# Splitting every whole-array product and transpose into two column halves

## The chip, the cores and the metric

One core of one Trainium2 chip runs the whole kernel in one launch. The metric is the device time of an execution in microseconds. Times of the kernel before are the median of three runs; the profile is of one further execution.

## What is computed

Retention-like attention (scores weighted by a power of a constant of each head, no softmax) over 8 batches, 8 heads, 576 positions and 64 numbers a head, and on its output a feed-forward layer with a SoLU activation and a normalisation over 1024 hidden columns:

```python
scores = scale * np.matmul(q, k.transpose(0, 1, 3, 2))
gamma = 1.0 - 2.0 ** (-5.0 - np.arange(H))
Dmat = np.where(rel >= 0, gamma[:, None, None] ** rel, 0.0)
attn = np.matmul(scores * Dmat, v)            # -> x: 4608 tokens x 512

h = x @ w_in                                   # 512 -> 1024
e = np.exp(h - h.max(-1, keepdims=True))
solu = h * e / (e.sum(-1, keepdims=True) + 1e-9)
ln = (solu - mu) / np.sqrt(var + 1e-6) * g_ln
out = ln @ w_out                               # 1024 -> 512
```

## The kernel before

**Tiles.** The 4608 tokens are 36 chunks of 128. A batch is four chunks and half of a fifth; the fifth of two batches share one chunk, so every ninth chunk is such a shared one. The decay is split into a factor of the row and one of the column, which are multiplied into q and v, and a chunk's past comes from a running state of 64 x 64 numbers a head, so that a chunk needs its own scores and one product with the state.

**Steps.** Each chunk n passes through small functions with names of two letters. Those of TensorE are:

- `tq`, `tr` (L232, L256): transposes of q, and of k in early chunks, 128 x 128 each, into PSUM (`tp`, `tr`); later chunks have k transposed by a DMA (`kd`, L241)
- `sc` (L290): scores, two heads at a time, each in one half of the array's rows (operands of 64 partitions)
- `kv` (L314) and `av` (L365): the state's new part `kp`, and scores times v, `x`; two heads at a time, each in one half of the array's columns (outputs of 64 partitions). These two already have the form that the change gives to others
- `fs` (L380): adds the product of q with the state to `x`
- `m1`, `mr` (L412, L400): `h`, 8 matmuls of 512 columns in two accumulations of four
- `tu` (L495): 8 transposes of the activated `u` into `lp`
- `m2` (L515): `o`, 8 matmuls of 512 columns in one accumulation
- `hm`, `ht`, `h2` (L538, L588, L619): the last chunk's `h`, transposes and `o`, in two parts each; `mm` (L721) a mean over w_out, `wu` (L645) four matmuls ahead of use

The others: POOL scales and converts q, v and k (L210, L199, L171) and makes the state in two forms (`dk` L341, `d3` L353), and computes the normalisation's factor `rs` (L477 to L487). VectorE adds to the state (`ad`, `t`, L327 and L329), masks the scores (`ret`, L303), takes the maximum (`nm`, L422) and forms `u` (L437). ScalarE copies out of PSUM (L171), takes the exponential (`e`, L428), squares (`sq`, L465) and scales the output (`o_sb`, L523).

**Order.** Nothing is scheduled by a planner: three strings of tokens (START, LOOP, END) name the steps in program order, and each engine takes its own in that order. LOOP stands for one step of a software pipeline over the chunks; on TensorE it runs `tr` (chunk + 2), `tu` (- 2), `m1`, `kv` (+ 1), `av` (+ 1), `sc` (+ 2), `fs` (+ 1), `m2` (- 2). A fourth string, BANKS, says which of four PSUM banks each product takes; `h` has two buffers of its own. SP's queue issues the loads some six chunks ahead, the stores, and the DMA transposes.

Of the kernel before, what the change touches and what calls it, by code (L numbers as in the profile page):

```python
# [13 lines left out]
P = 128  # L14
# [79 lines left out]
def kernel(  # L94
# [10 lines left out]
    nc = tc.nc  # L105
# [3 lines left out]
    NF = DFF // P  # L109
# [35 lines left out]
    ident = const.tile([P, P], F16, name="ident")  # L145
    mhalf = const.tile([P, 1], FP, name="mhalf")
    warm = const.tile([P, 512], F16, name="warm")
    ones = const.tile([P, P], F16, name="ones")
# [5 lines left out]
    w_in16 = const.tile([P, 4, DFF], F16, name="w_in16")  # L154
    w_out16 = const.tile([P, NF, DM], F16, name="w_out16")
# [8 lines left out]
    def bank(shape, dtype, name):  # L164
        return ps.tile(shape, dtype, tag="b" + next(banks), name=name)

    ENG = {"a": nc.scalar, "v": nc.vector, "g": nc.gpsimd}
    T = {}
# [2 lines left out]
        (engine.copy if engine is nc.scalar else engine.tensor_copy)(out=out, in_=in_)  # L171


    def quads(n):

        return n != NCH - 2

    def ld(n):

        for key, src in (("qf", q), ("kf", k), ("vf", v)):  # L180
            dst = load.tile([P, H, D], FP, name=key, bufs=6 if key == "kf" else 7)
            for pp, b, s0 in rows(n):
                m = pp.stop - pp.start
                if key == "qf" and quads(n):
                    nc.sync.dma_start(
                        out=dst[pp].rearrange("p (h a) d -> p h (a d)", h=2),
                        in_=src[b, :, s0 : s0 + m, :].rearrange(
                            "(g h) (t a) d -> t g h (a d)", h=2, a=4
                        ),
                    )  # L190
                    continue
                nc.sync.dma_start(
                    out=dst[pp], in_=src[b, :, s0 : s0 + m, :].rearrange("h p d -> p h d")
                )
            T[key, n] = dst
# [9 lines left out]
    def cq(n, e="g"):  # L205
        if not quads(n):
            return scaled(n, "qf", "q16", gq, ENG[e])
        table = gqm if chunks[n][1] == 4 else gqt
        dst = half.tile([P, H, D], F16, name="q16", bufs=5)
        ENG[e].tensor_tensor(  # L210
            out=dst.rearrange("p (a h) d -> p h a d", h=2),
            in0=T.pop(("qf", n)).rearrange("p (h a) d -> p h a d", h=2),
            in1=table.rearrange("p (h a) -> p h a", h=2).unsqueeze(3).to_broadcast([P, 2, 4, D]),
            op=ALU.mult,
        )
        T["q16", n] = dst
# [9 lines left out]
    def tq(n):  # L226

        tp = bank([P, 2, 4, P], F16, "tp")
        for i, src in enumerate((T.pop(("q16", n)), T["k16", n])):
            s2 = src.rearrange("p h d -> p (h d)")  # L230
            for hp in range(4):
                nc.tensor.transpose(  # L232
                    out=tp[:, i, hp], in_=s2[:, hp * P : (hp + 1) * P], identity=ident
                )
        T["tp", n] = tp

    def kd(n):
# [12 lines left out]
    def tr(n):  # L250
        if chunks[n][1] == 4 or n < BY_DMA:
            return tq(n)
        tp = bank([P, 4, P], F16, "tr")
        s2 = T.pop(("q16", n)).rearrange("p h d -> p (h d)")
        for hp in range(4):
            nc.tensor.transpose(  # L256
                out=tp[:, hp], in_=s2[:, hp * P : (hp + 1) * P], identity=ident
            )
        T["tp", n] = tp

    def er(n, e="a"):
# [4 lines left out]
    def turned(engine, n, out, tp):  # L266

        if not quads(n):
            return copy(engine, out, tp)
        copy(  # L270
            engine, out.rearrange("p g (t a) -> p g t a", a=4),
            tp.rearrange("p a (t g) -> p g t a", g=4),
        )
# [98 lines left out]
    def fs(n):  # L372

        bs, c = chunks[n]
        qkT = T.pop(("qkT", n))
        s16 = [T.pop(("s16", b, c)) for b in bs] if c > 0 else []
        w = P // len(bs)
        for hp in range(4):
            for i, s in enumerate(s16):
                nc.tensor.matmul(  # L380
                    out=T["x", n][:, hp, i * w : (i + 1) * w],
                    lhsT=s[:, hp].rearrange("p e d -> p (e d)"),
                    rhs=qkT[:, 0, hp, i * w : (i + 1) * w],
                    start=False, stop=i == len(s16) - 1, skip_group_check=True,
                )
        T["xs", n] = T.pop(("x", n))

# [5 lines left out]
    def mr(n, d):  # L393

        d = int(d)
        done = T.get(("rows", n), 0)
        if done == 0:
            T["h", n] = ps_h.tile([P, DFF], FP, tag="h", name="h")
        for i in range(2):
            nc.tensor.matmul(  # L400
                out=T["h", n][:, i * 512 : (i + 1) * 512], lhsT=T["xT", n][:, d],
                rhs=w_in16[:, d, i * 512 : (i + 1) * 512], start=done == 0, stop=done == 3,
            )
        T["rows", n] = done + 1

    def m1(n):

        xT = T.pop(("xT", n))
        h = ps_h.tile([P, DFF], FP, tag="h", name="h")
        for i in range(2):  # L410
            for d in range(4):
                nc.tensor.matmul(  # L412
                    out=h[:, i * 512 : (i + 1) * 512], lhsT=xT[:, d],
                    rhs=w_in16[:, d, i * 512 : (i + 1) * 512], start=d == 0, stop=d == 3,
                )
        T["h", n] = h

    def mx(n):
# [71 lines left out]
    def tu(n):  # L490

        u = T.pop(("u", n))
        lp = bank([P, NF, P], F16, "lp")
        for c in range(NF):
            nc.tensor.transpose(out=lp[:, c], in_=u[:, c * P : (c + 1) * P], identity=ident)  # L495
        T["lp", n] = lp

    def du(n):
# [9 lines left out]
    def m2(n):  # L508

        uT = T.pop(("uT", n))  # L510
        o = bank([P, DM], FP, "o")
        assert T["w_out"] == NF and (n < PLAIN or T["w_cen"] == NF)
        w = w_out16 if n < PLAIN else T["w_c"]
        for c in range(NF):
            nc.tensor.matmul(  # L515
                out=o, lhsT=uT[:, c], rhs=w[:, c], start=c == 0, stop=c == NF - 1
            )
        T["o", n] = o

    def st(n):  # L520
# [10 lines left out]
    def hm(n, i):  # L531

        if i == "0":
            T["hx", n] = T.pop(("xT", n))
        i = int(i)
        h = bank([P, 512], FP, "hh")
        for d in range(4):
            nc.tensor.matmul(  # L538
                out=h, lhsT=T["hx", n][:, d], rhs=w_in16[:, d, i * 512 : (i + 1) * 512],
                start=d == 0, stop=d == 3,  # L540
            )
        T["hh", n, i] = h

    def hx(n, i):
# [38 lines left out]
    def ht(n, i):  # L583
        i = int(i)
        lp = bank([P, 4, P], F16, "lph")
        u = T.pop(("hu", n, i))
        for c in range(4):
            nc.tensor.transpose(out=lp[:, c], in_=u[:, c * P : (c + 1) * P], identity=ident)  # L588
        T["hlp", n, i] = lp

    def he(n, i, e="v"):
# [22 lines left out]
    def h2(n, i):  # L614

        w = slice(256 * int(i), 256 * int(i) + 256)
        o = bank([P, 256], FP, "oh")
        for c in range(NF):
            nc.tensor.matmul(  # L619
                out=o, lhsT=T["huT", n, c // 4][:, c % 4], rhs=T["w_c"][:, c, w], start=c == 0,  # L620
                stop=c == NF - 1,
            )
        T["ho", n, i] = o

    def hw(n, i, e):
# [15 lines left out]
    def wu(_, count):  # L641

        w = bank([P, 512], FP, "w")
        for _ in range(int(count)):
            nc.tensor.matmul(  # L645
                out=w, lhsT=warm[:, 0:P], rhs=warm, start=True, stop=True, skip_group_check=True
            )

    def c1(_):
        nc.scalar.dma_start(out=small, in_=nc.inline_tensor(small_np, name="small_c").ap())  # L650
# [65 lines left out]
    def mm(_):  # L716

        assert T["w_out"] == NF
        T["mean"] = bank([P, DM], FP, "mean")
        for c in range(NF):  # L720
            nc.tensor.matmul(  # L721
                out=T["mean"], lhsT=ones, rhs=w_out16[:, c], start=c == 0, stop=c == NF - 1
            )

    def mc(_, e):
        copy(ENG[e], warm, T.pop("mean"))
# [51 lines left out]
```

## Time and profile before

| | us |
|---|---|
| median of three runs (lowest, highest) | 217.87 (217.39, 219.24) |
| the profiled execution | 218.18 |
| its span in the profile | 216.5 |
| busy: PE, PE weight loads | 197.4, 110.8 |
| busy: DVE, ACT, POOL | 180.8, 167.1, 173.6 |

The profiled execution is 1.7 us longer than its span; that lies around the profiled part. PE is TensorE's matmuls, PEld its weight loads, which overlap the matmuls; DVE is VectorE, ACT ScalarE, POOL GpSimd, SP SyncE. A matmul's duration runs to the end of its drain, so matmuls of one group overlap in the rows: 128*128 with 512 columns lasts 379 ns, while the next one starts 216 ns after it. A shape such as 128*64 128x512 says that 128 rows and 64 columns of the array are used and that 512 columns are streamed.

### The profile page before, as it was taken

Reading aid. Unit: us, or ns where it says so; the run is one execution under the profiler, and the core shown is the slowest. Engines: PE = TensorE matmul, PEld = TensorE weight load, DVE = VectorE, ACT = ScalarE, POOL = GpSimd, SP = SyncE. Lnnn points to the kernel's source line nnn. Section 1 sums busy time; section 2 is a strip of 40 time slices with the busy share of each in tenths; the row PEclk is TensorE's granted clock in tenths of the full one; section 3 lists DMA queues with packets and bytes.
Section 4 is the critical chain, followed back from the end, with each engine's and each line's share of the span. In section 5 each row is a group of like instructions: output and inputs, shape, how many; then the busy total and the mean of one; then the engine's idle time right before and its main releaser. Section 6 shows DMA issues by size and latency. Waiting matters only on the chain.

```text
span 216.5 us, 5376 instructions
## 1 busy us (share of the span) xinstructions
PE 197.4 (91%) x1989; PEld 110.8 (51%) x1989; DVE 180.8 (84%) x289; ACT 167.1 (77%) x279; POOL 173.6 (80%) x275
## 2 busy tenths in 40 slices
PE   0379889896999999999999999999999999999993
PEld 0254456453455555555555555555555565545451
DVE  1378899999997998888888898888888999889840
ACT  2073988966897888888888788888888794986991
POOL 3348889997367899999997899999997899977340
PEclk9999999999999999999999999999999999999999
DMA  5999999998986899799999998899999999674845
GB/s 137 289 317 287 228 280 358 193 245 224 270 228 168 219 183 201 177 225 258 243 223 232 255 208 186 186 247 248 214 227 213 253 181 190 145 172 100 195 109 182
DMA packets 112250, 47.04 MB, mean 217 GB/s; under 512 B 96984, under 2 KB 106208, under 8 KB 112224
## 3 DMA queue, kind: packets, MB, share of 16 engines
q1 hardware_dynamic: 111904, 46.55, 92.7%
q8 instruction: 15, 0.25, 0.5%
q10 hardware_dynamic: 320, 0.16, 0.3%
q14 instruction: 11, 0.09, 0.2%
HBM read 32.54 MB, written 9.44 MB: 194 GB/s over the span
## 4 chain that ended last, share of the span: by engine, by line
PE 78%; DVE 13%; DMA 2%; issue 2%; SPq 2%; ACT 1%; DVEq 0%; ACTq 0%
PE o L515 26%; PE h L412 23%; PE sc L290 5%; PE lp L495 5%; PE x L365 4%; PE x L380 3%; PE kp L314 3%; DVE nm L422 3%; DVE ret L303 2%; DMA vf<-in_v_dram 2%; PE tp L232 2%; PE tr L256 2%; PE h L400 2%; DVE u L437 2%; DVE q L210 1%
## 5 line engine op out<-in xcount | busy, mean ns | idle before, releaser
L412 PE MATMUL h<-w_in,xT 128*128 128x512 f16 x264 | 62.4, 379 | 0.5 <-DVE u L437 0.5
L515 PE MATMUL o<-w_c,uT 128*128 128x512 f16 x240 | 56.5, 379 | 0.6 <-DVE t L327 0.4
L428 ACT ACTIVATE e<-h,nm 128x1024 f32<-128x1024 f32 x35 | 39.0, 1116 | 14.0 <-DVE nm L422 14.0
L303 DVE TENSOR_TENSOR ret<-sc,tris 128x512 f16<-128x512 f32 x72 | 46.1, 682 | 1.3 <-PE sc L290 1.2
L437 DVE SCALAR_TENSOR_TENSOR u<-h,e 128x1024 f16<-128x1024 f32 x35 | 42.7, 1220 | 2.7 <-ACT e L428 1.4
L422 DVE TENSOR_REDUCE nm<-h 128x1 f32<-128x1024 f32 x35 | 42.5, 1216 | 2.0 <-PE h L412 1.5
L515 PEld LDWEIGHTS <-uT 128*128 128x128 f16 x280 | 26.2, 98 | 27.1 <-issue 0.4
L412 PEld LDWEIGHTS <-xT 128*128 128x128 f16 x264 | 24.2, 98 | 24.4 <-issue 0.5
L341 POOL TENSOR_TENSOR s<-t,small 128x512 f16<-128x512 f32 x32 | 34.2, 1070 | 2.6 <-DVE t L329 2.6
L199 POOL TENSOR_TENSOR v<-vf,small 128x512 f16<-128x512 f32 x32 | 33.6, 1051 | 3.0 <-DMA vf<-in_v_dram 3.0
L465 ACT ACTIVATE sq<-u,su 128x1024 bf16<-128x1024 f16 x30 | 34.8, 1159 | 0.1
L210 POOL TENSOR_TENSOR q<-qf,small 128x512 f16<-128x512 f32 x30 | 31.3, 1044 | 1.8 <-DMA qf<-in_q_dram 1.8
L171 ACT CAST xT<-x 128x512 f16<-128x512 f32 x34 | 19.9, 585 | 11.1 <-PE x L380 10.6
L523 ACT ACTIVATE o_sb<-o,rs 128x512 f32<-128x512 f32 x35 | 23.9, 685 | 4.1 <-POOL rs L487 1.6
L171 ACT COPY uT<-lp 128x1024 f16<-128x1024 f16 x25 | 25.3, 1012 | 0.3 <-PE lp L495 0.2
L487 POOL TENSOR_TENSOR rs<-w,mhalf 128x1 f32<-128x1 f32 x36 | 19.8, 551 | 3.0
L483 POOL TENSOR_SCALAR w<-ss,w 128x1 f32<-128x1 f32 x31 | 8.9, 287 | 15.9 <-ACT sq L465 13.9
L171 POOL CAST k<-kf 128x512 f16<-128x512 f32 x28 | 17.1, 611 | 3.0 <-DMA kf<-in_k_dram 3.0
L171 ACT COPY qkT<-tp 128x512 f16<-128x512 f16 x20 | 10.7, 594 | 10.9 <-PE tp L232 10.9
L495 PE MATMUL lp<-ident,u 128*128 128x128 f16 x224 | 17.0, 219 | 1.3 <-DVE u L453 1.3
L353 POOL TENSOR_TENSOR s<-t,small 128x256 f32<-128x256 f32 x24 | 14.9, 622 | 3.4 <-DVE t L327 2.5
L290 PE MATMUL sc<-qkT 64*128 64x128 f16 x288 | 15.2, 225 | 2.0 <-ACT qkT L171 1.2
(89 smaller groups left out, 262.5 us busy)
## 6 DMA issues: line engine op xcount, KB each, us to landing
qf<-in_q_dram SPq DMA_DIRECT2D x32, 256.0 KB, 4.0
kf<-in_k_dram SPq DMA_DIRECT2D x32, 256.0 KB, 4.4
vf<-in_v_dram SPq DMA_DIRECT2D x32, 256.0 KB, 4.7
out_dram<-o_sb SPq DMA_DIRECT2D x32, 256.0 KB, 2.6
w_in<-in_moe_w_in_dram SPq DMA_DIRECT2D x4, 512.0 KB, 6.1
w_out<-in_moe_w_out_dram SPq DMA_DIRECT2D x4, 512.0 KB, 6.7
qf<-in_q_dram SPq DMA_DIRECT2D x8, 128.0 KB, 3.2
kf<-in_k_dram SPq DMA_DIRECT2D x8, 128.0 KB, 3.8
```

Of the source, the lines that this page charges most:

```text
L171: (engine.copy if engine is nc.scalar else engine.tensor_copy)(out=out, in_=in_)
L199: engine.tensor_tensor(out=dst, in0=T.pop((key, n)), in1=table.unsqueeze(2).to_broadcast([P, H, D]), op=ALU.mult,)
L210: ENG[e].tensor_tensor(out=dst.rearrange("p (a h) d -> p h a d", h=2), in0=T.pop(("qf", n)).rearrange("p (h a) d -> p h a d", h=2), in1=ta ...
L303: nc.vector.tensor_tensor(out=r, in0=s, in1=m, op=ALU.mult)
L341: nc.gpsimd.tensor_tensor(out=s16, in0=t.unsqueeze(2).to_broadcast([P, 4, 2, D]), in1=gd.unsqueeze(3).to_broadcast([P, 4, 2, D]), op=ALU.mult,
L412: nc.tensor.matmul(out=h[:, i * 512 : (i + 1) * 512], lhsT=xT[:, d], rhs=w_in16[:, d, i * 512 : (i + 1) * 512], start=d == 0, stop=d == 3,)
L422: nc.vector.tensor_reduce(out=nm, in_=T["h", n], axis=AX.X, op=ALU.max, negate=True)
L428: nc.scalar.activation(out=e, in_=T["h", n], func=ACT.Exp, bias=T.pop(("nm", n)), accum_out=s)
L437: nc.vector.scalar_tensor_tensor(out=u, in0=T.pop(("h", n)), scalar=-1.0, in1=T.pop(("e", n)), op0=ALU.mult, op1=ALU.mult, accum_out=su,)
L465: nc.scalar.activation(out=s, in_=T.pop(("v", n)), func=ACT.Square, scale=-float(DFF), bias=T.pop(("su", n)), accum_out=ss,)
L495: nc.tensor.transpose(out=lp[:, c], in_=u[:, c * P : (c + 1) * P], identity=ident)
L515: nc.tensor.matmul(out=o, lhsT=uT[:, c], rhs=w[:, c], start=c == 0, stop=c == NF - 1)
```

## The change

Two helpers are new, and every product and transpose that used 128 columns of the array goes through them. The first issues a transpose as two, for the left and the right 64 columns of its input; the second issues a matmul as two, for the left and the right 64 columns of the stationary operand, with the same moving operand. Each writes 64 partitions of the same PSUM tile. The helpers turn 1156 matmuls into 2312, and as many weight loads; `sc`, `kv`, `av` and the one small transpose of g_ln are left. Nothing changes on another engine, nor in the order of the steps.

```diff
+    HALF = (slice(0, 64), slice(64, P))
+
+    def turn(out, in_):
+        for w in HALF:
+            nc.tensor.transpose(out=out[w], in_=in_[:, w], identity=ident)
+
+    def product(out, lhsT, rhs, start, stop):
+        for w in HALF:
+            nc.tensor.matmul(
+                out=out[w], lhsT=lhsT[:, w], rhs=rhs, start=start, stop=stop,
+                skip_group_check=True,
+            )
...
     def tq(n):
-                nc.tensor.transpose(
-                    out=tp[:, i, hp], in_=s2[:, hp * P : (hp + 1) * P], identity=ident
-                )
+                turn(tp[:, i, hp], s2[:, hp * P : (hp + 1) * P])
...
     def m1(n):
         for i in range(2):
             for d in range(4):
-                nc.tensor.matmul(
-                    out=h[:, i * 512 : (i + 1) * 512], lhsT=xT[:, d],
-                    rhs=w_in16[:, d, i * 512 : (i + 1) * 512], start=d == 0, stop=d == 3,
-                )
+                w = slice(i * 512, (i + 1) * 512)
+                product(h[:, w], xT[:, d], w_in16[:, d, w], d == 0, d == 3)
...
     def m2(n):
         for c in range(NF):
-            nc.tensor.matmul(
-                out=o, lhsT=uT[:, c], rhs=w[:, c], start=c == 0, stop=c == NF - 1
-            )
+            product(o, uT[:, c], w[:, c], c == 0, c == NF - 1)
...
```

`tr`, `fs`, `mr`, `tu`, `hm`, `ht`, `h2`, `wu` and `mm` are changed in the same way.

More of the change, by code (lines that the diff above doesn't have):

```diff
@@ L255, in tr @@
         for hp in range(4):
-            nc.tensor.transpose(
-                out=tp[:, hp], in_=s2[:, hp * P : (hp + 1) * P], identity=ident
-            )
+            turn(tp[:, hp], s2[:, hp * P : (hp + 1) * P])
         T["tp", n] = tp
@@ L379, in fs @@
             for i, s in enumerate(s16):
[L380 to L384, printed above, removed]
+                at = slice(i * w, (i + 1) * w)
+                product(
+                    T["x", n][:, hp, at], s[:, hp].rearrange("p e d -> p (e d)"),
+                    qkT[:, 0, hp, at], False, i == len(s16) - 1,
                 )
@@ L399, in mr @@
         for i in range(2):
-            nc.tensor.matmul(
-                out=T["h", n][:, i * 512 : (i + 1) * 512], lhsT=T["xT", n][:, d],
-                rhs=w_in16[:, d, i * 512 : (i + 1) * 512], start=done == 0, stop=done == 3,
-            )
+            w = slice(i * 512, (i + 1) * 512)
+            product(T["h", n][:, w], T["xT", n][:, d], w_in16[:, d, w], done == 0, done == 3)
         T["rows", n] = done + 1
@@ L411, in m1 @@
             for d in range(4):
-                nc.tensor.matmul(
-                    out=h[:, i * 512 : (i + 1) * 512], lhsT=xT[:, d],
-                    rhs=w_in16[:, d, i * 512 : (i + 1) * 512], start=d == 0, stop=d == 3,
-                )
+                w = slice(i * 512, (i + 1) * 512)
+                product(h[:, w], xT[:, d], w_in16[:, d, w], d == 0, d == 3)
         T["h", n] = h
@@ L494, in tu @@
         for c in range(NF):
-            nc.tensor.transpose(out=lp[:, c], in_=u[:, c * P : (c + 1) * P], identity=ident)
+            turn(lp[:, c], u[:, c * P : (c + 1) * P])
         T["lp", n] = lp
@@ L514, in m2 @@
         for c in range(NF):
-            nc.tensor.matmul(
-                out=o, lhsT=uT[:, c], rhs=w[:, c], start=c == 0, stop=c == NF - 1
-            )
+            product(o, uT[:, c], w[:, c], c == 0, c == NF - 1)
         T["o", n] = o
@@ L537, in hm @@
         for d in range(4):
[L538 to L541, printed above, removed]
+            w = slice(i * 512, (i + 1) * 512)
+            product(h, T["hx", n][:, d], w_in16[:, d, w], d == 0, d == 3)
         T["hh", n, i] = h
@@ L587, in ht @@
         for c in range(4):
-            nc.tensor.transpose(out=lp[:, c], in_=u[:, c * P : (c + 1) * P], identity=ident)
+            turn(lp[:, c], u[:, c * P : (c + 1) * P])
         T["hlp", n, i] = lp
@@ L618, in h2 @@
         for c in range(NF):
[L619 to L622, printed above, removed]
+            product(o, T["huT", n, c // 4][:, c % 4], T["w_c"][:, c, w], c == 0, c == NF - 1)
         T["ho", n, i] = o
@@ L644, in wu @@
         for _ in range(int(count)):
-            nc.tensor.matmul(
-                out=w, lhsT=warm[:, 0:P], rhs=warm, start=True, stop=True, skip_group_check=True
-            )
+            product(w, warm[:, 0:P], warm, True, True)
     def c1(_):
@@ L720, in mm @@
         for c in range(NF):
-            nc.tensor.matmul(
-                out=T["mean"], lhsT=ones, rhs=w_out16[:, c], start=c == 0, stop=c == NF - 1
-            )
+            product(T["mean"], ones, w_out16[:, c], c == 0, c == NF - 1)
     def mc(_, e):
```

## The prediction

> **What bounds the kernel now.** I read the page's busy table and chain first, then the stretches, then one step of the loop in order of time, then the groups by line.
>
> ```profile
> PE 197.4 (91%) x1989; PEld 110.8 (51%) x1989; DVE 180.8 (84%) x289; ACT 167.1 (77%) x279; POOL 173.6 (80%) x275
> ...
> PE 78%; DVE 13%; DMA 2%; issue 2%; SPq 2%; ACT 1%; DVEq 0%; ACTq 0%
> ```
>
> TensorE is 78% of the chain that ended last. By stretches (columns: stretch, its length, then busy time of PE, PEld, DVE, ACT, POOL, granted clock, DMA share, GB/s) the start belongs to VectorE and all behind it to TensorE:
>
> ```profile
> 20.00:52.00 32.00, 27.32 (x275) 15.64 (x274) 31.29 (x48) 25.49 (x45) 29.93 (x40) 1.00 1.03 253
> ...
> 100.00:165.00 65.00, 64.55 (x679) 36.49 (x674) 56.69 (x87) 54.06 (x86) 59.91 (x94) 1.00 1.00 223
> 165.00:212.00 47.00, 46.78 (x434) 25.07 (x432) 39.95 (x67) 38.63 (x71) 35.73 (x63) 1.00 0.84 178
> ```
>
> In the waits between 66 and 165 us no wait of PE is longer than 0.4 us. So what is worth something is time in TensorE's own stream from 52 us on. One step of the loop, PE alone (start, duration to the end of the last matmul, line, tile, shape, count):
>
> ```profile
> 134.48 1.89 PE L412 MATMUL h<-w_in,xT 128*128 128x512 f16 x8
> 136.30 0.32 PE L314 MATMUL kp<-v,k 128*64 128x64 f16 x8
> 136.45 0.39 PE L365 MATMUL x<-ret,v 128*64 128x128 f16 x8
> 136.78 0.40 PE L290 MATMUL sc<-qkT 64*128 64x128 f16 x8
> 137.11 0.40 PE L380 MATMUL x<-qkT,s 128*128 128x128 f16 x4
> 137.34 1.89 PE L515 MATMUL o<-w_c,uT 128*128 128x512 f16 x8
> 139.07 0.39 PE L256 MATMUL tr<-ident,q 128*128 128x128 f16 x4
> 139.29 0.28 PE L495 MATMUL lp<-ident,u 128*128 128x128 f16 x2
> ```
>
> Two things are to be seen. First, **column halves already run side by side here**: the eight half-width matmuls of L365 (128*64, 128 columns streamed) take 0.39 us, exactly what four whole-width ones of the same length take in L256. Less the 0.22 us of the last matmul's own duration that is about 0.17 us for three steps, 56 ns each for one whole matmul or for a pair of halves. Second, **a change of the array's shape costs time**. The groups o and tr have one shape, and tr starts 139.07 - 137.34 = 1.73 us after o, which is 8 matmuls at 216 ns. kp has another shape than h, and starts 136.30 - 134.48 = 1.82 us after it: 0.09 more for the same work. x to sc and sc to L380 are 0.33 us each where 4 steps of 56 ns make 0.22: 0.1 us each. L380 to o, again one shape, is 0.23. So a step of 5.25 us (131.05 to 136.30 by the start of kp) has three changes of shape, near 0.3 us in all.
>
> **The change, part by part.**
>
> *Work streamed: 0.* Of 1989 matmuls 1156 become 2312, each with its own weight load; a loop step goes from 56 matmuls to 88. If a pair of halves takes what one whole matmul takes, h and o stay 8 x 216 ns, tr, lp and L380 stay 56 ns a pair. For 128 columns L365 is the direct row. For 512 columns no row has halves. The bounds are 0 and, if the second half ran behind the first, another 216 ns for each; I take 0, since L365 is two halves with two different moving operands at the full rate, and a longer stream only repeats that.
>
> *Weight loads: 0.* The loads become those of the other form:
>
> ```profile
> L412 PEld LDWEIGHTS <-xT 128*128 128x128 f16 x264 | 24.2, 98 | 24.4 <-issue 0.5
> L365 PEld LDWEIGHTS <-v 128*64 128x64 f16 x288 | 9.9, 113 | 3.6 <-issue 2.9 <-DVE ret L303 0.4
> ```
>
> 113 ns against 98, so 15 ns more each. In L365 two such loads lie under each 56 ns pair and nothing of them shows; under 216 ns there is more cover still. Were the cover gone, the 16 short pairs of a step that take this form anew (L380, tr, lp) would show 16 x 15 ns = 0.24 us, more than the change can bring. The Trainium skill (TensorEngine Tiling, Restrictions and Gotchas) says that column tiling and the fast weight load exclude each other. By that rule, with nothing to cover the slower loads, 0.24 - 0.09 = 0.15 us would be lost in each of some 31 steps, about 222.5 us; by the row of L365, none. I go by the row.
>
> *Changes of shape: the gain.* After the change everything but sc (64*128) has the one shape 128*64. h to kp, and x to L380 where no sc stands between, lose their change; x to sc, sc to L380, h or o to sc keep theirs, as sc keeps its own shape. In the order of the two programs 120 changes of shape become 71: the 49 between whole width and half width go. Placed on the timeline, 15 of the 49 lie before 52 us and 34 behind. One of these (171.62) ends in a wait for VectorE and brings nothing. The others: 33 x 0.093 us = 3.1 us. In the start VectorE is busy 31.3 of 32 us, so there I take 0 (bounds 0 and 15 x 0.1 = 1.5 us).
>
> *Who could take the time back.* The removed 0.09 us lies ahead of kp. From kp to o nothing changes, so the tight loop kp, VectorE's t, o's bank, which leaves o only some 0.1 us of room, keeps its length. VectorE waits about 0.6 us for kp in a step, ScalarE as much for x. POOL is the close one. Its own step on the timeline, from one scaling of v to the next:
>
> ```profile
> 130.70 1.04 POOL L199 TENSOR_TENSOR v<-vf,small 128x512 f16<-128x512 f32 x1
> ...
> 136.10 1.04 POOL L199 TENSOR_TENSOR v<-vf,small 128x512 f16<-128x512 f32 x1
> ```
>
> 5.40 us, over PE's 5.25: it falls behind by 0.15 us a step and makes it up at every ninth chunk, which leaves out L341 and L353. In the waits between 66 and 165 us its longest entry is this (us in total, times, longest):
>
> ```profile
> POOL w L483 <- ACT sq L465: 4.7, 6, 1.2
> ```
>
> Over the nine steps from 110.07 to 157.54 (47.47 us) it waits for sq 1.09, 0.59 and 0.19 us, so it needs 45.6; nine faster steps offer 47.47 - 0.84 = 46.6. That fits, with half of its spare time gone. DMA is loaded (share 1.00), but SP's queue waits for POOL's casts and for o_sb, not for bytes. I take off 0.1 us for steps near the end where something else is late by less than 0.09.
>
> **Sum.** 3.1 - 0.1 = 3.0 us. The profiled execution took 218.18 us: 216.5 of span and 1.7 around it. Its span becomes 213.5, its time 215.2; it lies 0.3 above the median of 217.87, so I predict a median of 214.9, 1.4% below. (About 1% is what a measurement of this kernel can tell from no change.)
>
> **The rivals.**
>
> *POOL, not PE, sets the step.* If its lag of 0.15 us grows to 0.24 and reaches rs for ScalarE's o_sb or s for L380 before the ninth chunk, half the gain is lost: 216.4. For it: 60 of 65 us busy. Against: the nine-step budget above. If all is lost, or the 0.09 us at kp is not the shape but something that stays, 217.9. Against that: the extra stands at every change of shape and at no other seam of the step.
>
> *The instruction stream becomes the bound (slower).* A step has 112 loads and matmuls in 5.25 us now, 47 ns each, and PE doesn't starve; it would have 176 in 5.16, 29.3 ns each. That is the point from which it decides: a front end that needs more than 29.3 ns per instruction sets the step. The rows bound it by 47 from above and by L314 and L365 from below: 32 instructions from 136.30 to 136.78, 15 ns each, though these may have been queued beforehand. At 31 ns a step is 5.46 us, 31 steps (160 us at 5.25) lose 0.21 each, so 217.9 + 6.5 = 224.4; at 47 it is 8.3 us, and some 310. For it: no stretch of this trace holds 29 ns for 5 us. Against: the sequencer gets far enough ahead that kp, x and sc together run without a gap. The Trainium skill (TensorE: Matmul & The Clock Gate, "Wait — 56ns, not 53.3ns?") gives 62 ns of the sequencer per MATMUL where the hardware decoder is off; 88 of them would be an estimated 5.46 us a step, and the time 224.
>
> *Two streams of 512 columns hinder each other (slower).* Behind 52 us there are 496 products of 512 columns; 3.1 us are gone at 6.3 ns each, 3% of 216. At 10% it is 496 x 22 ns = 10.9 us, less the gain, 225.7; at the bound, 325. Against: L365.
>
> **Chances.** Forecast 0.64 (its own range 213.3, all 49 changes at 0.093 us gained, to 215.7); POOL or the same seam 0.17; instruction stream 0.11; hindered streams 0.08. Faster by over 1% (below 215.7): 0.64. Within 1%: 0.16, most of the second case. Slower: 0.20, the last two rivals and a rest. The low end is 213.3; the high end 219.5 holds the second case whole and the mildest of the last two, and leaves out less than 2 in 10.
>
> **What would show it.** Right: h to kp is 1.73 us by starts, a step 5.16, o and h still start their pairs 216 ns apart, x to sc and sc to L380 still 0.33; POOL's waits for sq shrink to about half. Wrong: pairs of h or o more than 222 ns apart (hindered streams); gaps in PE put down to issue in lp, tr or kp while the pairs of o are right (front end); PE waiting for DVE t or POOL s, with h to kp at 1.73 (POOL).

## The result, and the profile after

The changed kernel takes 219.89 us in the median of 14 runs (218.65 to 221.35), the kernel before 218.0 beside it (216.75 to 220.31). The ratio is 1.0096, with a 95% interval of 1.0069 to 1.0124: slower by 1%, where 1.4% faster was forecast. Here and below a median is of all executions, while the ratio and its interval leave out those more than 1.5% above the fastest of their kernel, so kernels are compared by the ratios. The profiled execution of after took 219.48 us, with a span of 217.8.

TensorE did its part. One step of the loop in after, PE alone (start, duration to the end of the last matmul, line, tile, shape, count, and in brackets what it waited for):

```profile
130.60 1.89 PE L184 MATMUL h<-w_in,xT 128*64 128x512 f16 x16
132.33 0.29 PE L325 MATMUL kp<-v,k 128*64 128x64 f16 x8
132.45 0.39 PE L376 MATMUL x<-ret,v 128*64 128x128 f16 x8
132.78 0.40 PE L301 MATMUL sc<-qkT 64*128 64x128 f16 x8
133.10 0.41 PE L184 MATMUL x<-qkT,s 128*64 128x128 f16 x8
133.35 1.89 PE L184 MATMUL o<-w_c,uT 128*64 128x512 f16 x16
135.08 0.39 PE L179 MATMUL tr<-ident,q 128*64 128x128 f16 x8
135.30 0.61 PE L179 MATMUL lp<-ident,u 128*64 128x128 f16 x16
135.75 1.89 PE L184 MATMUL h<-w_in,xT 128*64 128x512 f16 x16
137.47 0.29 PE L325 MATMUL kp<-v,k 128*64 128x64 f16 x8
137.60 0.39 PE L376 MATMUL x<-ret,v 128*64 128x128 f16 x8
140.03 0.40 PE L301 MATMUL sc<-qkT 64*128 64x128 f16 x8 [2.04 <-DMA qkT<-k]
```

(The helpers stand at L179 and L184, so every transpose bears the one line and every split product the other.) Sixteen halves of `h` take 1.73 us to the start of `kp`, where eight whole ones took 1.82; `o` to `tr` is 1.73 as before; a step is 135.75 - 130.60 = 5.15 us. Then, in the next step, `sc` stands still for 2.04 us because k, which a DMA transposes, has not come. In the waits of before between 66 and 165 us there was no such entry; here it has two (us in total, times, longest), one for the weight load and one for the matmul:

```profile
PEld L301 <- DMA qkT<-k: 3.8, 3, 2.2
PE sc L301 <- DMA qkT<-k: 3.3, 2, 2.0
```

The chain that ended last now has DMA and SP's queue in it, 11% and 4% where both had 2%, and the stretches show it (columns: stretch, its length, busy time of PE, PEld, DVE, ACT, POOL, granted clock, DMA share, GB/s):

```profile
PE 63%; DMA 11%; DVE 10%; POOL 4%; SPq 4%; ACT 3%; issue 3%; POOLq 0%; DVEq 0%; ACTq 0%
```

```profile
66.00:100.00 34.00, 33.97 (x580) 22.84 (x581) 30.91 (x47) 28.64 (x47) 32.34 (x51) 1.00 0.97 213
100.00:165.00 65.00, 61.19 (x1040) 40.31 (x1038) 54.51 (x85) 52.50 (x84) 58.32 (x91) 1.00 1.02 215
```

From 100 to 165 us PE is busy 61.2 us where it had 64.55; DMA is at 1.02, and VectorE, ScalarE and POOL are less busy than before. Up to 100 us nothing is lost.

The starts of `sc` say where. In the traces the time goes by (us; the loop's steady part is from chunk 12 to 33, the end follows):

| kernel | `sc` of chunk 12 | 12 to 33 | 33 to 35 | 35 to the span's end | span |
|---|---|---|---|---|---|
| before | 78.80 | 107.17 | 9.15 | 21.4 | 216.5 |
| after | 75.81 | 110.15 | 9.91 | 21.9 | 217.8 |

After is 3.0 us ahead at chunk 12 and 4.0 at chunk 23 (132.78 against 136.78). It loses 2.0 of that at chunk 24 and 1.25 at chunk 25, each to a wait for k, is level at chunk 33 (185.96 and 185.97), and 1.3 behind at the end. The last 1.1 ahead of chunk 33 goes to a late load: ScalarE stands still for 4.04 us until `kf` is there, makes `o_sb` late, and `tr` waits 1.19 us for that, at 183.89.

**The start.** That after was ahead at chunk 12 was not in the sum either. Before, TensorE waited 1.9 us at 52.05 for a copy that VectorE made late. VectorE's rows ahead of it, before and then after:

```profile
45.75 1.09 DVE L453 TENSOR_SCALAR u<-u,nmu 128x1024 f16<-128x1024 f16 x1
46.76 1.53 DVE L210 TENSOR_TENSOR q<-qf,small 128x512 f16<-128x512 f32 x1
48.21 2.04 DVE L730 TENSOR_TENSOR w_c<-w_out,warm 128x512 f16<-128x512 f16 x3
```

```profile
44.65 0.49 DVE L459 TENSOR_SCALAR u<-u,nmu 128x1024 f16<-128x1024 f16 x1
45.05 0.69 DVE L225 TENSOR_TENSOR q<-qf,small 128x512 f16<-128x512 f32 x1
45.65 1.09 DVE L725 TENSOR_TENSOR w_c<-w_out,warm 128x512 f16<-128x512 f16 x3
```

The same three groups take 4.66 us and 2.27. In before POOL runs a cast of k and two products (L341, L199) beside them, from 44.94 to 47.7; in after POOL waits for kf until 46.36. So the start depends on how the two engines' rows happen to overlap.

**SP's queue** is where k gets late. Its rows in before (start, duration, line, what it issues):

```profile
127.51 1.96 SPq L241 DMA_TRANSPOSE qkT<-k  x1
129.61 1.19 SPq L528 DMA_DIRECT2D out_dram<-o_sb  x2
130.84 1.26 SPq L185 DMA_DIRECT2D qf<-in_q_dram  x2
132.15 1.31 SPq L192 DMA_DIRECT2D kf<-in_k_dram  x2
133.50 1.31 SPq L192 DMA_DIRECT2D vf<-in_v_dram  x2
134.98 2.11 SPq L241 DMA_TRANSPOSE qkT<-k  x1
```

and in after:

```profile
127.54 2.76 SPq L254 DMA_TRANSPOSE qkT<-k  x1
130.40 1.19 SPq L532 DMA_DIRECT2D out_dram<-o_sb  x2
131.63 1.26 SPq L200 DMA_DIRECT2D qf<-in_q_dram  x2
132.94 1.31 SPq L207 DMA_DIRECT2D kf<-in_k_dram  x2
134.30 2.55 SPq L207 DMA_DIRECT2D vf<-in_v_dram  x2
137.01 1.22 SPq L254 DMA_TRANSPOSE qkT<-k  x1
```

In both the queue runs back to back here: it goes from one issue to the next and waits for no engine. From 100 to 144 us no gap between two of its rows is over 0.2 us in either kernel. The transpose for chunk 24 has its data when POOL's cast ends, 129.74 in before and 126.57 in after, and issues at 134.98 and at 137.01. It lands at 139.06, with 2.97 us to spare until `sc` starts, and at 139.99, with 0.04 (a `sc` that waits for k starts 0.04 to 0.05 us after the landing). Nor does any of the 21 transposes of k in before wait for its data: each cast had ended 0.9 to 6.5 us before the issue. From 66 to 100 us SP's rows fill 29.5 of 34 us before and 31.3 after. Before keeps a lead all along (2.6 to 6.1 us, most over 3.5). From chunk 12 to 24 it shrinks from 6.09 to 2.97 us there; in after from 4.28 to 0.04, and `sc` has waited 2.04 besides. So after loses 4.24 + 2.04 - 3.12 = 3.2 us more of lead. 1.05 of this is TensorE, which gets there faster; the other 2.1 are transposes that land later than in before by the distance of the two chunks (68.46 us between the two landings, where before has 66.35). In this pair of traces the transfers aren't only asked for sooner: they come more slowly.

### The profile page after: what moved, and what is told of

The parts are those of the page before. It is cut to its first block, busy times and chain, and to the rows that moved or that the text cites. A ratio compares the mean times of both kernels' runs of the same rounds, so it can differ in the third digit from the quotient of the medians.

```text
span 217.8 us, 7689 instructions
## 1 busy us (share of the span) xinstructions
PE 194.3 (89%) x3145; PEld 127.3 (58%) x3145; DVE 178.3 (82%) x289; ACT 166.1 (76%) x279; POOL 173.6 (80%) x275
## 4 chain that ended last, share of the span: by engine, by line
PE 63%; DMA 11%; DVE 10%; POOL 4%; SPq 4%; ACT 3%; issue 3%; POOLq 0%; DVEq 0%; ACTq 0%
PE h L184 22%; PE o L184 21%; DMA qkT<-k 5%; PE lp L179 5%; PE sc L301 4%; DMA vf<-in_v_dram 4%; DVE ret L314 3%; PE x L184 3%; PE tp L179 3%; PE x L376 2%; DVE u L443 2%; DMA uT<-u 2%; DVE nm L428 2%; SPq L207 2%; SPq L200 2%
## 5 line engine op out<-in xcount | busy, mean ns | idle before, releaser
L184 PE MATMUL h<-w_in,xT 128*64 128x512 f16 x560 | 67.6, 382 | 0.6 <-DVE u L443 0.5
L184 PE MATMUL o<-w_c,uT 128*64 128x512 f16 x480 | 57.1, 380 | 1.2 <-DVE t L338 0.4
L184 PEld LDWEIGHTS <-xT 128*64 128x64 f16 x576 | 33.1, 110 | 22.1 <-issue 1.1
L184 PEld LDWEIGHTS <-uT 128*64 128x64 f16 x560 | 32.1, 110 | 23.0 <-issue 0.8
L352 POOL TENSOR_TENSOR s<-t,small 128x512 f16<-128x512 f32 x32 | 33.7, 1054 | 1.3 <-DVE t L340 1.3
L171 ACT CAST xT<-x 128x512 f16<-128x512 f32 x34 | 19.9, 585 | 13.4 <-PE x L184 13.1
L179 PE MATMUL lp<-ident,u 128*64 128x128 f16 x448 | 17.3, 219 | 1.0 <-DVE u L459 1.0
L179 PEld LDWEIGHTS <-q 128*64 128x64 f16 x280 | 12.6, 114 | 9.4 <-issue 2.6
```

The lines of the kernel that those rows point to most:

```text
L179: nc.tensor.transpose(out=out[w], in_=in_[:, w], identity=ident)
L184: nc.tensor.matmul(out=out[w], lhsT=lhsT[:, w], rhs=rhs, start=start, stop=stop, skip_group_check=True,)
L352: nc.gpsimd.tensor_tensor(out=s16, in0=t.unsqueeze(2).to_broadcast([P, 4, 2, D]), in1=gd.unsqueeze(3).to_broadcast([P, 4, 2, D]), op=ALU.mult,
```

## The experiments

Theory: the DMA side (its engines near a share of 1.00, with the loads and the transposes of k in one queue) delivers no faster than before needed, so a faster step only makes k late. The rivals are named with the runs. All ratios are to the kernel before, with a 95% interval.

### Room on the DMA side: v kept

In both kernels v of the chunks behind 12 isn't loaded: all use one tile.

```diff
+            if key == "vf" and n > VRES:      # VRES = 12
+                T[key, n] = v_kept
+                continue
...
```

> The kernel before with v loaded no more behind chunk 12 (later chunks use chunk 12's v): 256 KB and one DMA issue less a step. A control. Both theories: TensorE's stream bounds it and is not touched, so 216.5 to 218.

> The changed kernel with the same v kept. Theory 1: with room on the DMA side the shorter TensorE step comes through, 213 to 215, at least 2.5 us below the kernel before with v kept, and sc no longer waits for qkT. Theory 2: the slower DMAs cost less with less to move, but no gain, 217 to 219.

Before with v kept: 217.98 us, 0.9969 (0.9922 to 1.0015). After with v kept: 215.59, 0.9913 (0.9877 to 0.9949). Room on the DMA side is worth nothing that shows to the kernel before, and it turns the changed one round: its interval lies below the kernel before, and its ratio 1.8% below that of after. The distance of the two kernels with v kept is 0.6%, 1.2 us, less than the 2.5 us expected, and their intervals overlap; what the halves gain there is read from the traces. No wait for k is left in its list of waits, and the loop is full again at a DMA share of 0.77:

```profile
100.00:165.00 65.00, 64.51 (x1090) 42.70 (x1086) 57.52 (x89) 55.34 (x88) 61.08 (x97) 1.00 0.77 178
```

Chunks 12 to 33 take 105.43 us, against 107.17 in before with v kept: 1.74 us for 21 steps, 0.083 a step. Between 124 and 145 us each transpose holds SP's queue for 1.21 to 1.23 us, in both kernels; with v loaded it is 1.2 to 3.6.

### A faster step without halves

The last of the eight matmuls of `o` is left out from chunk 5 on, in the kernel before and in the changed one.

```diff
-        for c in range(NF):
+        m = NF if n < PLAIN else NF - 1
+        for c in range(m):
...
```

> The kernel before (whole-width products), with the last of the eight matmuls of o left out from chunk 5 on: 31 x 0.216 = 6.7 us less of TensorE's stream, no change of shape and no DMA touched. Theory 1, the DMA side (SP's queue of issues, its transposes held up by loaded DMA engines) sets the pace as soon as a TensorE step is shorter than about 5.25 us: 216 to 219, at most a third of the 6.7 us comes out, and sc waits for qkT. Theory 2, the halves themselves slow the DMAs (each half reads the moving operand again, and there is more code to fetch): whole-width products do not, so most of it comes out, 211.5 to 214.

> The changed kernel with the last of the eight products of o left out from chunk 5 on, as before_7of8 (216.3) leaves it out of the whole-width kernel. TensorE's step is then far below what the DMA side can feed in both, so what differs is what the halves do to the DMA side itself. Theory 1 (the DMA side alone sets the pace, halves or not): within 1 us of 216.3, and clearly below the 219.9 of the changed kernel or level with it by the same waits for qkT. Theory 2 (halves slow the DMAs once these are the limit): 218.5 to 220.5.

Before: 216.32 us, 0.9894 (0.9827 to 0.996). After: 218.87, 1.0015 (0.9968 to 1.0063). Of some 6.7 us of matmuls taken out of TensorE, 2.3 come out of the whole-width kernel by its ratio. So a shorter step alone, without a single half, runs into a limit too, and the time lies in the 216 to 219 of the first theory. It uses up the same lead: the transposes' time to spare falls from 5.6 us at chunk 12 to 0.05 at chunk 24. But the waits of `sc` for k that this theory named are not in its list between 66 and 165 us; what TensorE waits for there is POOL's s (0.8 us). The same cut in the changed kernel leaves it above, by intervals that just don't overlap, and there PE waits 5.0 us for k (in a profiled execution of 222.26, above its median). So the shorter step by itself doesn't make the whole difference.

With two of the eight left out (`NF - 2`):

> The kernel before with two of the eight matmuls of o left out from chunk 5 on: 13.4 us less of TensorE's stream. Theory 1: the DMA side is the limit already in before_7of8, so no more than 1.5 us below its 216.3; if running further ahead of the DMAs itself does harm (waits that delay what SP issues next), 217 to 220, above before_7of8. Theory 2: between 208 and 213.

> The changed kernel with two of the eight products of o left out from chunk 5 on; its whole-width partner before_6of8 took 214.6. TensorE's step is near 4.7 us in both, so the DMA side sets the pace in both and what differs is what the halves do to it. If they do nothing: 213.5 to 215.5. If they slow it: 217 to 220, and the loads of q from the 18th to the 38th on SP's queue take over 91.5 us (88.4 in before_6of8).

Before: 214.57 us, 0.9863 (0.9812 to 0.9914), with no wait of PE for k. After: 218.23, 0.9929 (0.9866 to 0.9992, from three of six executions), with waits for k of 3.7 us on the matmul and 6.1 on the weight load. The same order again, though here the intervals overlap.

That the whole-width kernel gets so little out of 13.4 us has another reason, which the waits of this before show (66 to 165 us; us in total, times, longest):

```profile
ACT o_sb L524 <- POOL rs L487: 5.6, 7, 1.0
PE sc L290 <- ACT uT L171: 1.6, 5, 0.4
PE x L380 <- POOL s L341: 0.9, 2, 0.4
```

POOL is busy for 62.4 of the 65 us from 100 to 165, and chunks 12 to 33 take 104.48 us, 4.98 a step (5.00 with 7 of 8). The prediction's budget for POOL was 45.6 us for nine steps, 5.07 each. So in these two whole-width kernels it is POOL, and ScalarE behind it, that stops a faster step; their partners with halves wait for k.

### SP's queue: its order, and another queue for the stores

The transposes of k go ahead of the loads in each step of LOOP (all else as in after):

```diff
-tr:2 so:-1 tu:-2 ld:6 er:2:v m1:0 dk:0 kv:1 eu:-2:a kd:4 ad:1 ...
+tr:2 so:-1 tu:-2 kd:4 ld:6 er:2:v m1:0 dk:0 kv:1 eu:-2:a ad:1 ...
```

> The changed kernel with the DMA transpose of k (kd) ahead of the three loads in each step of the loop instead of behind them; the same DMAs in another order on SP's queue. Theory 1: sc's transposes come some 2 us earlier, the loads have lead enough, 216 to 218. Theory 2: the order matters little, 219 to 220.5.

220.26 us, 1.0123 (1.0066 to 1.018): no gain, as the second case had it; the first is a miss. The transposes come in time and hold SP for 1.26 us in the median, but the loads behind them are late in their place (POOL waits 5.4 us for kf). This order of the queue only changed which transfer is late.

The stores go from SP's queue to ScalarE's:

```diff
-            nc.sync.dma_start(out=out[...], in_=o_sb[pp])
+            nc.scalar.dma_start(out=out[...], in_=o_sb[pp])
```

> The changed kernel with the stores of o_sb issued on ScalarE's queue instead of SP's: some 0.58 us a step less for SP, the same bytes, packets and transposes. If SP's time to issue is what binds on the DMA side: 215.5 to 217.5, as with v kept. If it is the DMA engines (SP being held up in its transposes because they are full): 219 to 221.

224.11 us, 1.0228 (1.0156 to 1.03): a miss for both sides. ScalarE itself stalls at the issues (behind most its copy of uT is 0.4 us late, behind one at 104.28 1.73). Its one trace, of an execution of 227.12, shows more than the time does. No wait of PE for k is left between 66 and 165 us: k lands 5.0 to 8.0 us before its use, at a DMA share of 1.08, and chunks 12 to 33 take 108.71 us (after 110.15). Most of what it loses stands in START (`sc` of chunk 12 at 83.43). That points to SP's time to issue, more than to full DMA engines, as what makes k late; but ScalarE is slowed in the same run, so it isn't settled.

### Four transposes given back to TensorE

k of the chunks 14, 20, 23 and 29 is transposed by TensorE, as k of the early chunks is; the whole computation is done.

```diff
-        if chunks[n][1] == 4 or n < BY_DMA:
+        if chunks[n][1] == 4 or n < BY_DMA or n in BY_PE:   # BY_PE = (14, 20, 23, 29)
```

> The changed kernel with four of the DMA transposes of k (chunks 14, 20, 23 and 29) given back to TensorE: 4 x 0.21 us more of products and four copies more on VectorE, four DMA transposes less on SP's queue. Theory 1: SP gains 4 x 1.3 to 3 us, the waits of sc for qkT go, 215.5 to 217.5. Theory 2: 218.5 to 220, since the loads are as slow as before.

> The kernel before with the same four transposes of k (chunks 14, 20, 23, 29) given back to TensorE as in after_fewer (215.8). If the gain of after_fewer comes from the halves, once the DMA side has room, this is slower than before by the 4 x 0.22 us on TensorE: 218 to 219.5. If it comes from the transposes given back alone: 215.5 to 217.

With halves: **215.78 us, 0.9937 (0.9899 to 0.9974)**, below both kernels. Without: 218.93, 1.0061 (1.0027 to 1.0095). These two intervals lie well apart, by 1.2%, 2.7 us. TensorE does four chunks' transposes more in each, and it costs the whole-width kernel 0.6%. With halves the same work pays, because no `sc` waits for k any more:

```profile
100.00:165.00 65.00, 64.90 (x1130) 43.43 (x1126) 58.16 (x91) 55.94 (x89) 61.25 (x94) 1.00 1.01 225
```

Chunks 12 to 33 take 105.96 us against 107.70 without halves: 1.74 us, the same as with v kept.

### What puts after above before, and not level with it

**Smaller matmuls or more of them?** `h` and `o` as two whole-width matmuls of 256 columns each, in the kernel before with 7 of 8 and with 6 of 8; and halves in `m1` and `m2` alone, or in the transposes and `fs` alone, with 6 of 8.

```diff
-                    out=h[:, i * 512 : (i + 1) * 512], lhsT=xT[:, d],
...
+                for j in (512 * i, 512 * i + 256):
...
+                        out=h[:, j : j + 256], lhsT=xT[:, d], rhs=w_in16[:, d, j : j + 256],
...
```

> before_7of8 with each 512-column product of h and o of the loop issued as two whole-width ones of 256 columns: as many more instructions and weight loads as the halves bring for these products, and the same streamed columns, moving operands read once. If the code to be fetched (or the number of instructions) is what slows the DMAs: 218.5 to 220.5. If it is the second reading of the moving operand, or nothing of the split at all: 215.5 to 217.

> before_6of8 with the same products m1 and m2 issued as two whole-width ones of 256 columns: the same 486 more matmuls and loads as half512_6of8, moving data read once. If the code is what costs: level with half512_6of8, 1 to 2 us over before_6of8 (214.6). If the second reading is: within 0.7 us of before_6of8.

217.69 us, 0.9966 (0.9921 to 1.0012) with 7 of 8, between its two neighbours (0.9894 and 1.0015) and apart from neither; and 215.83, 0.984 (0.9769 to 0.991) with 6 of 8, level with the whole-width kernel's 0.9863. The first decides nothing. By the second ratio the additional matmuls and loads of `h` and `o` cost nothing, but it comes from three of six executions, and both traces point the other way: the weight load of `sc` waits for k, 0.4 us with 7 of 8 and 3.1 with 6 of 8 (an execution of 219.46, above its median), where the kernels with 512 columns show no such wait. So these two runs leave open whether the number of matmuls makes k late.

```diff
-                product(h[:, w], xT[:, d], w_in16[:, d, w], d == 0, d == 3)
+                halves(h[:, w], xT[:, d], w_in16[:, d, w], d == 0, d == 3)
...
-            product(o, uT[:, c], w[:, c], c == 0, c == m - 1)
+            halves(o, uT[:, c], w[:, c], c == 0, c == m - 1)
```

(`halves` is the splitting helper; `product` and `turn` are whole width here.)

> The same with halves in the 512-column products m1 and m2 alone: 486 more matmuls with their loads, and nearly all of the moving data read twice. If the second reading slows the DMAs: as after_6of8. If it is the code to be fetched: some half of after_6of8's loss, level with the next two. TensorE's step gets two changes of shape more than whole width has (0.19 us), and is still under 5.05 us.

214.98 us, 0.9864 (0.9811 to 0.9918): level with 0.9863, with no wait of PE for k. Halves of the 512-column products alone, with their second reading of the moving operand, cost nothing that shows. The loss that they might have explained is small here, though: 0.9929 for all halves is not clear of 0.9864 either.

```diff
-                product(
+                halves(
                     T["x", n][:, hp, at], ...
```

(`turn` stays split; `m1` and `m2` are whole width.)

> before_6of8 with halves in the transposes and in fs alone: 562 more matmuls with their loads, little moving data read twice. If the code is what costs: 1 to 2.5 us over before_6of8. If the second reading is: within 0.7 us of before_6of8, or a little below by the changes of shape saved.

218.21 us, 1.0016 (0.9975 to 1.0057). Its step is 5.17 us with PE busy 64.5 of 65: TensorE is the bound again, since the small groups now have another shape than `h` and `o` and a step has six changes of shape. It shows once more that these cost time, but says little on the DMA side.

**Instruction fetches?** The instruction queue q8 in the profile's list of DMA queues has 15 packets before and 24 after, 16 KB each. Ten transfers of 16 KB, issued by ScalarE beside `sq` from chunk 12 to 30, were added to the kernel before with 6 of 8, and as a control ten of 64 B. (The expectation takes the DMA side for the limit of that kernel; its waits, above, name POOL.)

```diff
+        if 12 <= n < 32 and n % 2 == 0:
+            nc.scalar.dma_start(out=w_out32[0:1]...[:, 0:4096], in_=moe_w_in[0:4, :]...)   # or 0:16
```

> before_6of8 (214.6, whole width, the DMA side its limit) with ten more DMAs of one 16 KB row each, issued by ScalarE at every second chunk from 12 to 30: packets of the size in which the instructions of TensorE are fetched, and about as many as the halves add (24 against 15). If single packets of that size hold up the DMAs behind them on their engine, and so explain what the halves cost the DMA side: 2 us or more above its control with 64 bytes. If the fetches are harmless: within 0.7 us of the control.

> The control: the same ten DMAs at the same places with 64 bytes each. It differs from before_6of8 (214.6) only by ten issues on ScalarE: 214.3 to 216.

With 16 KB 216.54 us, 0.9941 (0.9902 to 0.998); with 64 B 214.27, 0.9813 (0.9756 to 0.987). In the two profiles, though, 2.3 us of the difference stand at chunk 12 (77.55 and 75.21), before any of the ten transfers, and from there to chunk 35 it is 114.34 against 113.56 us, 0.8 us. Halves cost 2.1 us there (115.51 after with 6 of 8, 113.41 before). So a few large packets may cost something beside a full DMA, less than is sought; that the fetches of after are what costs it there is not shown.

**The start alone, or the loop alone?**

```diff
+    part = list(HALF)              # start_only; the other: list(WHOLE)
...
-        for w in HALF:
+        for w in part:
...
         run(START, 0)
+        part[:] = WHOLE            # start_only; the other: HALF
```

> Halves in START alone (to the first step of the loop), whole width from there on; the whole computation. In the traces of the kernel before VectorE's u, q and w_c at 45.6 to 50.2 us take 1.09, 1.53 and 2.04 us beside POOL's work; in that of after they take 0.49, 0.69 and 1.09, and sc of chunk 7 stands at 51.51 instead of 54.32. Theory: the halves shift the two engines against each other, so the start is 2 to 3 us shorter here too; sc of chunk 12 at 75.8 to 76.8 (before 78.80), the loop at 5.25 us a step, 12 to 35 in 116.3 us, no wait for k of more than 0.3 us, and 215 to 216 us. Rival: the shorter start is chance, with no tie to the halves: sc of chunk 12 at 78.8, 217.5 to 218.5 us.

> Whole width in START, halves from the first step of the loop to the end; the whole computation. Theory: sc of chunk 12 at 78.8 as before, steps of 5.16 until the transposes of k are late; if the earlier start of after only used up the lead of SP's queue, that lead is 3 us larger here, the waits for k stay under 1 us in all, 12 to 35 takes 115 to 117 us and the time is 217 to 218.5. Rival: the halves themselves slow what SP's queue delivers, whatever the lead: waits for k as in after (3 us and more), 12 to 35 in 119 to 121 us, and 220 to 223 us.

Halves in START alone: 217.01 us, 0.9962 (0.9914 to 1.001). Halves behind START alone: 220.57, 1.0088 (1.0039 to 1.0138). (The profiled execution of the second took 223.32, so its trace stands above its median; it is read here for its waits.)

```profile
PEld L303 <- DMA qkT<-k: 2.7, 3, 1.4
PE sc L303 <- DMA qkT<-k: 2.2, 3, 1.2
```

Here the first theory fell in its second part. START whole leaves the loop with a lead of 5.1 us at chunk 12 (before 6.1, after 4.3), and k comes late all the same, so the loss doesn't come of the earlier start; what after loses, it loses behind START. In START the halves bring 1.2 us at chunk 12 (77.64), not the 2 to 3 expected; VectorE's three groups run at the short durations there.

The traces side by side, as in the table above:

| kernel | `sc` of chunk 12 | 12 to 33 | 33 to 35 | 35 to the span's end | span |
|---|---|---|---|---|---|
| before, v kept | 78.59 | 107.17 | 9.15 | 21.5 | 216.4 |
| after, v kept | 75.85 | 105.43 | 10.25 | 21.9 | 213.4 |
| before, four given back | 79.81 | 107.70 | 9.16 | 21.6 | 218.3 |
| after, four given back | 76.81 | 105.96 | 9.69 | 21.4 | 213.9 |
| before, 7 of 8 | 77.44 | 105.00 | 9.92 | 21.5 | 213.9 |
| halves in START alone | 77.64 | 107.17 | 9.16 | 21.3 | 215.3 |
| halves behind START alone | 79.87 | 109.47 | 9.92 | 22.3 | 221.6 |

## Why the prediction was wrong

**Work streamed, right.** Halves of 512 columns keep the pace: 1.73 us for eight pairs of `o`, as for eight whole ones. The rival of two streams that hinder each other is out.

**Weight loads and instruction stream, right.** The loads of a half last 110 ns in `h` and nothing of them shows; the 16 loads and 16 matmuls of `lp` take 0.45 us to the start of `h`, 56 ns for a pair of halves. The Trainium skill's rule that column tiling and the fast weight load exclude each other (TensorEngine Tiling, Restrictions and Gotchas) agrees with the longer loads, 110 ns against 98, but the loss worked out from it had no place in this stream. The 62 ns of the sequencer per MATMUL that the Trainium skill gives for a hardware decoder that is off (TensorE: Matmul & The Clock Gate, "Wait — 56ns, not 53.3ns?") are not seen: 16 matmuls of `lp` pass in 0.45 us, 28 ns each.

**Changes of shape, right in the loop.** 0.093 us each was the price; `h` to `kp` came out as 1.73, the step as 5.15 instead of 5.16. Where the DMA side has room, 21 steps gain 1.74 us, 0.083 a step, in two independent pairs of kernels, one trace each.

**The start, mis-sized.** It was taken at 0, bounds 0 to 1.5. The trace of after has 3.0 us at chunk 12, and halves in START alone 1.2. Most of it is VectorE's 2.4 us, which hang on when POOL's rows fall beside its own. The trace of the 64 B control, whole-width throughout START, has the early start too (75.21 at chunk 12), so it isn't the halves' alone. They seem to make it more frequent: with halves in START chunk 12 stands at 75.8 to 77.6 in seven traces (83.43 in the eighth, with the stores on ScalarE), without at 75.2 to 79.9 in ten.

**Who could take the time back: the step that failed.** It looked at VectorE, ScalarE and POOL, and dismissed DMA with "SP's queue waits for POOL's casts and for o_sb, not for bytes". The SP rows of before show the opposite: the cast of chunk 24 had ended 5.2 us before its transpose was issued, and the queue ran back to back, as it did ahead of every transpose of k. The list of SP's waits does name POOL, but also rows on which no transpose of k depends (w, s, q), so the cast's end had to be held against the issue. In after PE waits 3.6 us for k between chunks 12 and 33, and that is where the gain went: 107.17 less the 1.74 that the halves bring, plus 3.6 for k and 1.2 for `tr`, is 110.2 us, and 110.15 was measured. POOL, which the prediction called the close one, didn't become the bound here (its waits for sq went from 4.7 us to 4.3, not to half); it is the next one, as the runs with 7 and 6 of 8 at whole width show. The sum had no term for the lead of k's transposes, which had already shrunk to 3 us in the kernel before, nor for a delivery that gets slower (3.2 us of lead lost, 1.05 of it by the faster step). The two rivals that are slower were both on TensorE; none was on the transfers, though the DMA share of 1.00 stood in a line that was shown.

**What is shown and what isn't.** That the transfers take the gain is shown by the waits for k and by two ways of making room, which take the waits away and bring a gain back: by the ratios 1.2 us with v kept, with intervals that overlap, and 2.7 us with four given back, with intervals apart. In the traces the spans differ by 3.0 and 4.4 us. Only part of that is the loop's 1.74; START gives about 3 us in these traces, and the end takes 0.3 to 1.5 back, where the chain goes through DMA-transposed q or u. Not shown is why the halves in the loop cost more than they gain once DMA is the limit: 219.89 against 218.0, and 220.57 with a start of whole width. Halves in `h` and `o` alone show no loss with 6 of 8, so their second reading is not it as far as these runs go; the number of matmuls and the instruction fetches remain possible. Against them as the only cause stands that with halves and 6 of 8 the transposes of chunk 12 to 24 are issued within 64.5 us (after 69.3, before 66.4), with the same code but for two products a chunk; an effect of where the transfers fall in time wasn't excluded.

## What to carry to other kernels

A shorter step on the engine that sets the pace is worth only what the next resource's lead allows, so for each transfer read its time to spare (landing to first use) and whether its queue waited for the data or the data for the queue. Where a DMA share is near 1.00, make room in the same change: four transposes given back to TensorE cost the slow step 0.6% and were worth 1.6% to the fast one (ratios 1.0096 and 0.9937). A list of a queue's waits can name a bystander, so compare the end of the data's last step with the issue. And a group's changes of array shape are worth counting: 0.08 to 0.09 us each here, so splitting only some of the products adds changes instead of removing them.

## What the hardware showed that was not expected

- A DMA transpose holds the queue that issues it: 1.2 us with room on the DMA engines (share 0.77), 1.2 to 3.6 us at a share of 1.00 to 1.02 behind three loads. The share alone doesn't set it: issued ahead of the loads it was 1.26 us in the median at a share of 1.06.
- Stores from ScalarE's queue in place of SP's cost 1.3%, 2.9 us (ratios 1.0228 and 1.0096), and ScalarE stalls at the issue (0.4 to 1.8 us in that trace).
- Some VectorE rows that write f16 take about twice as long beside POOL's cast and products (0.49 and 1.09 us for the same u, 0.69 and 1.53 for the same q); 2 to 3 us of the start hang on it, with the same instructions. Of the six traces looked at, three have the long rows (before, before with v kept, halves behind START) and three the short ones (after, the 64 B control, halves in START).
